# The dense stage of an attention and expert kernel on two scaled fp16 parts in place of float32r parts, always in pairs of token tiles

## The chip, the cores and the metric

The kernel runs on one core of a Trainium2 chip. The metric is device time in microseconds of one execution, as the median of several runs. The core's engines are PE (TensorE, matrix products; PEld is its weight load), DVE (VectorE), ACT (ScalarE), POOL (GpSimd) and SP (SyncE, which issues most transfers).

## What is computed

Three layers, one after the other, on 4 x 768 = 3072 tokens:

```python
# attention: 4 batches, 8 heads, 768 positions, 64 per head; a key is kept where it is one of the
# first 8, or lies less than 96 behind the query; ALiBi-like bias, softmax
x = attention(q, k, v)                                    # 3072 x 512
h = np.maximum(np.maximum(x @ w1, x @ w2), x @ w3)        # dense stage: 512 -> 768, three weights
x2 = h @ w_out                                            # 768 -> 512
e_idx = argmax(x2 @ w_gate)                               # one of 8 experts for each token
out = gate * sigmoid(x2 @ w_output_gate)[e_idx] * (relu(x2 @ w1[e_idx]) @ w2[e_idx])   # 512 -> 1024 -> 512
```

The dense weights w1, w2, w3 and w_out come as float64, so a row of weights is first put together to float32 by integer operations. All results must have about float32 accuracy. The kernel gets there with products of operands in two parts: x = xh + xl, w = wh + wl, and x w is taken as xh wh + xl wh + xh wl, three passes of the PE in place of one.

## The kernel before

A planner in Python (class `Plan`) writes the order of the work. Every piece of work is a generator that yields requests: `need` (facts that must hold), `take` (a free buffer of a kind), `op` (an instruction on an engine, with an estimated duration and the buffers that it reads and writes). `Plan.run` picks, again and again, the operation that can start earliest by its estimates, plus a hold time, ties by rank, and emits it. Each engine then runs its instructions in exactly this order, and the waits between engines follow from the data. A transfer is issued by SP in the same fixed order, with an estimated rate. If something comes later than estimated, the engine stands at it, whatever else would be ready.

The work in order of time:

- **Attention**, 24 units of 128 queries (`a_T`, `a_v`, `a_scores`, `a_trans`, `a_out`), up to about 467 us. A unit's result goes to memory (`xd`) in rows of one token tile (128 tokens).
- **Weight rows** (`load_row`, `convert`): 18 rows of 128 x 768 (w1, w2, w3) or 128 x 512 (w_out). A raw row is loaded straight to where the finished row will stand; two raw rows share a tile, so the finished parts can be written only when both partner rows have been read (`read`, m ^ 1). ACT scales the high words, DVE puts the bits together in three operations, ACT writes the high part, POOL the low part, both float32r (4 bytes).
- **Dense stage** (`m_load`, `m_1`, `m_max`, `m_2`): the first 16 token tiles go in eight pairs, the last 8 in two quads (four tiles). `m_load` loads a tile's x, transposes it on the PE and splits it (`split_T`: high part by ACT, low part by DVE). `m_1` makes the three products: in a pair each pass has 256 moving columns, in a quad 512; 216 passes for a pair, and 216 for a quad. `m_max` takes the banks: ACT copies the first product, DVE takes the maximum with the second and the third, then ACT and POOL or DVE split the hidden values into two parts. Three banks (`mbank`) are in turn. `m_2` multiplies with w_out, 18 passes of 512 columns for each tile. A pair's transposed x and hidden values have one buffer each (`xT`, `hh`); a quad's have one each too (`xTq`, `hhq`), in memory that is free only after attention (`open_m2`).
- **Routing** (`m_route`): a tile's expert choice, and an indirect transfer of its rows to the expert's region (`xs`). After 16 routed tiles `choose` fixes the order of the experts; when all 24 are routed, `lists` makes the lists of the loop. `pad_rows` writes twelve blocks of padding rows after attention.
- **Expert weights ahead of the loop** (`stage`, `split`): 16 pieces of 128 x 1024 float32 for the first two experts are loaded into staging buffers (`ws`) and split into fp16 parts, high part times 2^13 by ACT or DVE, low part by DVE. Two staging buffers exist at first; six more lie where w3 stood and come when the last `m_1` is through with w3 (`more_ws`). The finished parts of piece 4 and later lie where w1 and w2 stood, so their splits wait for the end of the last passes with w1 (pieces 4 to 9) or w2 (the rest).
- **Prologue and loop** (`pro_load`, `pro_1`, `pro_next`, `step`): the first 256 tokens of the first expert, with fp16 passes of 256 columns (L1631) and 512 (L1606), then a loop of 13 steps up to 957 us.
- **End**: a check over the collected range sums sets a flag; where it fails, `general_moe` computes all again in float32 (`tc.If(again > 0)`, L1862). `acc` holds sums of the low parts of the fp16 splits, `lows` the maxima of 64 columns of rows.

The shape of a dense pass, the lines that the change turns on:

```python
for d in range(KD):
    yield op(PE, pe(nt * P, 3), [xT, W_AT[j]], [bank])
    for n, (part, X) in enumerate(((0, xh), (0, xl), (1, xh))):
        nc.tensor.matmul(pj[:, f2, :], lhsT=w_at(j, part, d)[:, fs], rhs=X[:, d, :], ...)
```

Of the kernel before, what the change touches and what calls it, by code (L numbers as in the profile page):

```python
# [9 lines left out]
F32 = mybir.dt.float32  # L10
# [41 lines left out]
HS = 2.0**15  # L52
LOW = 2.0**-10
# [323 lines left out]
def local_attention_moe_kernel(  # L377
# [28 lines left out]
    NPAIR = NTILE // 2 - 4  # L406
    CHUNKS = [range(2 * c, 2 * c + 2) for c in range(NPAIR)] + [range(n, n + 4) for n in range(2 * NPAIR, NTILE, 4)]
    NCHUNK = len(CHUNKS)
# [14 lines left out]
    lows = cp.tile([P, NTILE + 6], F32, name="lows")  # L423
# [4 lines left out]
    hh_t = [mo.tile([P, KF, 2 * P], F32R, tag=f"hh{n}", name=f"hh{n}") for n in range(2)]  # L428
    WN = 2 * KD * FF
    WC = [FF, FF, FF, D]  # L430
    W_RAW, W_FIT = {}, {}
    for j in (0, 1, 2, 3):
        for n in range((KD if j < 3 else KF) // 2):
            W_RAW[j, n] = big.tile([P, 4 * WC[j]], F32, tag=f"w{j}{n}", name=f"raw{j}{n}")
    RAW = [W_RAW[j, c // 2][:, c % 2 * 2 * WC[j] : (c % 2 + 1) * 2 * WC[j]].bitcast(I32) for j, _, c in wrows]

    def w_at(j, part, c):
        if (j, c // 2) not in W_FIT:
            W_FIT[j, c // 2] = big.tile([P, 4 * WC[j]], F32R, tag=f"w{j}{c // 2}", name=f"w{j}{c // 2}")
        at_ = 2 * (c % 2) + part  # L440
        return W_FIT[j, c // 2][:, at_ * WC[j] : (at_ + 1) * WC[j]]
# [6 lines left out]
    with tc.manual_schedule(engines={mybir.EngineType.SP, mybir.EngineType.Activation}):  # L448
# [3 lines left out]
        for j, src in enumerate((q, k, v)):  # L452
# [7 lines left out]
            if j:  # L460
                _, w, c = wrows[j - 1]
                nc.sync.dma_start(out=RAW[j - 1], in_=w[c * P : (c + 1) * P, :].bitcast(I32))
# [130 lines left out]
    cp.tile([P, LINE // 2], F32, name="to_line")  # L593
    stock("hh", [hh_t])
# [102 lines left out]
    place = [Buf(t) for t in RAW]  # L697
    w_left = [KD, KD, KD, KF]

    def load_row(m):  # L700
        j, w, c = wrows[m]
        if m > 1:
            yield need(("row", m - 1), *([("k", ROW_LOAD[m])] if ROW_LOAD[m] >= 0 else []))
            yield dma(P * WC[j] * 8, [place[m - 2]], [place[m]])
            nc.sync.dma_start(out=RAW[m], in_=w[c * P : (c + 1) * P, :].bitcast(I32))
        state("row", m)
        plan.add(convert(m), (2, ROW_KEY[m], 9, m), HOLD_W if m < 2 * KD else HOLD_V)

    def convert(m):
# [4 lines left out]
        low, high = RAW[m][:, ::2], RAW[m][:, 1::2]  # L714
# [3 lines left out]
        yield op(ACT, act(n), [wt], [wb])  # L718
        nc.scalar.mul(out=wf, in_=high.bitcast(F32), mul=REBIAS)
# [1175 lines left out]
```

## Time and profile before

| what | value |
|---|---|
| time, median of 3 runs | 975.76 us (975.08 to 976.81) |
| the profiled execution: its time | 978.62 us |
| its span, first to last instruction | 977.1 us |
| PE busy | 897.1 us, 92% |
| PEld busy | 747.5 us, 77% |
| DVE busy | 678.2 us, 69% |
| ACT busy | 491.6 us, 50% |
| POOL busy | 223.0 us, 23% |
| mean granted PE clock | 0.968 |
| bytes moved | 160.9 MB, 165 GB/s |

How to read it: the shares are means over stages with different limits, so the stretches have to be looked at one by one. Matmuls are pipelined: a pass's record reaches from its start to its end, and the next one starts long before that, so the time that a pass costs is the distance from start to start in an unbroken burst, not its duration. The granted clock is the share of 2.4 GHz that the PE got; it has two levels, 1.0 and 0.5 (1.2 GHz). An engine's idle time is followed by the name of what ended it.

### The profile page before, as it was taken

The page shows a single profiled execution, that of the slowest core. Times are in us where ns is not written, and L with a number is a line of the kernel's source. Part 1 is how long each engine was busy: PE and PEld are TensorE (multiplying, and loading weights), DVE is VectorE, ACT ScalarE, POOL GpSimd, SP SyncE. Part 2 cuts the span into 40 slices and gives each one's busy share as a digit, 9 for nine tenths or more (in the row PEclk, how much of TensorE's full clock was granted, in tenths as well). Part 3 has the DMA queues.
Part 4 walks back from the last instruction along what each step waited for, and adds up shares of the span by engine and source line. Part 5 has one row for each costly group of instructions (what it writes and reads, how often), then busy time and mean ns, then how long its engine had stood idle before and what let it go on. Part 6 is the DMA issues. An engine that isn't in the chain of part 4 may idle for free. (4 is left out here: it accounts for less than half of the span.)

```text
span 977.1 us, 23443 instructions
## 1 busy us (share of the span) xinstructions
PE 897.1 (92%) x8305; PEld 747.5 (77%) x8305; DVE 678.2 (69%) x2101; ACT 491.6 (50%) x1070; POOL 223.0 (23%) x245
## 2 busy tenths in 40 slices
PE   2496898999899999999899998998999999999992
PEld 2385787998889898989778877777777777777770
DVE  6979876677768778776253535764777777777773
ACT  4767664676566656565121311332555444545551
POOL 3544322243222132120000010010222323222222
PEclk9997899999999999999899999998999999999996
DMA  7889286596875757664722102417777777776775
GB/s 207 234 221 235 57 154 131 132 170 139 159 143 113 162 130 158 137 137 100 200 92 60 33 33 74 142 44 248 223 227 229 240 240 238 239 251 218 224 228 185
DMA packets 222807, 160.90 MB, mean 165 GB/s; under 512 B 181344, under 2 KB 181344, under 8 KB 222724
## 3 DMA queue, kind: packets, MB, share of 16 engines
q1 hardware_dynamic: 218562, 147.23, 58.3%
q0 software_dynamic: 4160, 12.62, 3.4%
q8 instruction: 45, 0.74, 0.3%
q14 instruction: 38, 0.31, 0.1%
q10 hardware_dynamic: 2, 0.00, 0.0%
HBM read 118.56 MB, written 23.11 MB: 145 GB/s over the span
## 5 line engine op out<-in xcount | busy, mean ns | idle before, releaser
L1093 PE MATMUL bank<-xT,w 128*128 128x256 f32 x1728 | 234.8, 291 | 1.5 <-ACT xT L1037 1.0
L1093 PEld LDWEIGHTS bank<-xT,w 128*128 128x128 f32 x1728 | 217.9, 194 | 8.4 <-ACT xT L1037 3.2
L1606 PE MATMUL bank<-we,hE 128*128 128x512 f16 x672 | 147.3, 379 | 0.0
L1606 PEld LDWEIGHTS <-hE 128*128 128x128 f16 x672 | 65.7, 98 | 76.2
L950 ACT ACTIVATE sp<-sp,mn 128x232 f32<-128x232 f32 (+1 forms) x192 | 90.4, 472 | 53.1 <-DVE mn L943 46.4
L1093 PE MATMUL bank<-wq,w 128*128 128x512 f32 x432 | 103.7, 400 | 3.1 <-DVE hm L1115 3.1
L1595 ACT ACTIVATE hm<-bank 128x512 f32<-128x512 f32 x56 | 33.4, 597 | 140.1 <-PE bank L1652 94.3
L1093 PEld LDWEIGHTS bank<-wq,w 128*128 128x128 f32 x432 | 82.3, 193 | 20.7 <-DVE hm L1115 3.5
L198 DVE SCALAR_TENSOR_TENSOR we<-ws_more,we 128x1024 f16<-128x1024 f32 x81 | 96.9, 1222 | 0.2
L1115 DVE TENSOR_TENSOR hm<-hm,bank 128x512 f32<-128x512 f32 x72 | 49.4, 686 | 64.5 <-PE bank L1093 63.9
L1255 POOL DMA_INDIRECT xs<-x2r,di x24 | 24.8, 1032 | 281.0 <-DVE x2r L1252 150.2
L1529 ACT ACTIVATE we<-ws_more 128x1024 f16<-128x1024 f32 x80 | 79.9, 1047 | 0.3 <-DMA ws_more<-in_moe_w_dram 0.3
L1153 PE MATMUL bank<-w,hh 128*128 128x512 f32 x288 | 78.1, 417 | 0.0
L1652 PEld LDWEIGHTS <-we 128*128 128x128 f16 x1248 | 73.1, 100 | 5.2 <-ACTq L1835 2.0
L1652 PE MATMUL bank<-xE,we 128*128 128x128 f16 x1248 | 74.4, 222 | 2.0 <-DVE xE L198 1.8
L1652 PE MATMUL bank<-xE,wp 128*128 128x128 f16 x1248 | 71.8, 219 | 0.0
L1652 PEld LDWEIGHTS <-wp 128*128 128x128 f16 x1248 | 70.8, 98 | 0.1
L943 DVE CUSTOM_DVE_ANT_0 sp<-bank,bias 128x232 f32<-128x232 f32 x160 | 60.1, 389 | 11.4 <-PE bank L919 11.0
L820 POOL TENSOR_SCALAR qkn<-qkn,vs 128x512 f32<-128x512 f32 x23 | 38.2, 1662 | 118.9 <-DVE vs L815 50.0
L919 PE MATMUL bank<-k,qh 64*128 64x232 f32 (+1 forms) x384 | 44.5, 321 | 20.8 <-ACT k L893 17.4
L1153 PEld LDWEIGHTS bank<-w,hh 128*128 128x128 f32 x288 | 54.1, 198 | 10.6
L193 POOL TENSOR_TENSOR seen<-wf,dco 128x1 f32<-128x1 f32 x14 | 13.2, 940 | 199.7 <-DVE wf L1611 199.7
(276 smaller groups left out, 1526.4 us busy)
## 6 DMA issues: line engine op xcount, KB each, us to landing
ws_more<-in_moe_w_dram SPq DMA_DIRECT2D x87, 512.0 KB, 4.0
bias<-in_moe_w_dram SPq DMA_DIRECT2D x21, 512.0 KB
ws<-in_moe_w_dram SPq DMA_DIRECT2D x20, 512.0 KB
raw<-in_moe_w_dram SPq DMA_DIRECT2D x12, 768.0 KB
x2r<-xs SPq DMA_DIRECT2D x30, 257.0 KB, 2.7
qkn<-in_q_dram SPq DMA_DIRECT2D x23, 256.0 KB
qkn<-in_k_dram SPq DMA_DIRECT2D x23, 256.0 KB
qkn<-vd SPq DMA_DIRECT2D x23, 256.0 KB
```

The costliest lines, as they stand in the source:

```text
L198: nc.vector.scalar_tensor_tensor(out=out, in0=x, scalar=scale, in1=high, op0=ALU.mult, op1=ALU.subtract, accum_out=total)
L820: nc.gpsimd.tensor_scalar(out=vf, in0=vf, scalar1=scale, scalar2=None, op0=ALU.mult)
L919: nc.tensor.matmul(sc[j][:, hp, :nw_], lhsT=x, rhs=y, start=(n < 2), stop=(n >= len(terms) - 2))
L943: nc.vector.tensor_tensor_reduce(out=o[:, g:], in0=x[:, g:], in1=bias[:, pr, n0 + g :], scale=scale, scalar=low, op0=ALU.add, op1=ALU.min, ...
L950: nc.scalar.activation(out=o, in_=o, func=AF.Exp, scale=-1.0, bias=mn[:, h : h + 1], accum_out=sm[:, h : h + 1])
L1093: nc.tensor.matmul(pj[:, f2, :], lhsT=w_at(j, part, d)[:, fs], rhs=X[:, d, :], start=(d + n == 0), stop=(d == KD - 1 and n == 2))
L1115: nc.vector.tensor_max(out=hv, in0=hv, in1=pj)
L1153: nc.tensor.matmul(bank.t, lhsT=X[:, f, t * P : (t + 1) * P], rhs=w_at(3, part, f), start=(f + n == 0), stop=(f == KF - 1 and n == 2))
L1529: nc.scalar.mul(out=h, in_=s.t, mul=XS)
L1595: nc.scalar.activation(out=rows, in_=bank.t, func=AF.Relu, scale=HS / XS**2)
L1606: nc.tensor.matmul(py, lhsT=at(A_), rhs=w, start=(f + m == 0), stop=(last and m == 2))
L1652: nc.tensor.matmul(pg[:, f, :], lhsT=W[d][B_][:, fs], rhs=xT[A_][:, d, :], start=(d + m == 0), stop=(d == KD - 1 and m == 2))
```

## The change

- The dense stage's operands are fp16 parts: x times 2^13 (`XS`), the weights times 2^16 (`WS`), hidden values times 2^13. The three passes per product stay. The evictions take the scale out again: ACT's copies become scaled copies, DVE's maximum becomes one operation with a scale and a maximum. The low part of x comes from `low_of`, which leaves a sum beside it.
- All 24 tiles go in pairs: twelve pairs, no quads, no `xTq` and `hhq`. fp16 takes half the room: `xT` and `hh` become two buffers each. The last pair runs in the same order as the others.
- Finished weight rows have a place of their own (`W16`). Raw rows go through a ring of eight buffers (`raw`); a row waits until the buffer of the eighth row before it has been read. Partner rows don't wait for each other.
- The fp16 parts of the 16 expert pieces lie in the ring's memory (24 half pieces) and in `wp0` (8), so their splits need no dense weight to be done with. Nine staging buffers (`ws`) from `open_m2` on; `more_ws` goes. `stage` waits for the issue of the last x load as well.
- `pro_1` puts its hidden values where w1 stood and waits for the last `m_1`.
- Range checks: for each weight row DVE takes the largest magnitude of the finished high part (`widest`, after attention unit 6 + m mod 6), ACT's first step takes an absolute value with a sum; for each x tile DVE takes a maximum over 64 columns. All sums lie in one tile, `chk`; the final check has four more DVE operations.
- The branch to `general_moe` gets `preferred_fallthrough_block=False`.

```diff
-    NPAIR = NTILE // 2 - 4
-    CHUNKS = [range(2 * c, 2 * c + 2) for c in range(NPAIR)] + [range(n, n + 4) for n in range(2 * NPAIR, NTILE, 4)]
+    NCHUNK = NTILE // 2
+    CHUNKS = [range(2 * c, 2 * c + 2) for c in range(NCHUNK)]
...
-    hh_t = [mo.tile([P, KF, 2 * P], F32R, tag=f"hh{n}", name=f"hh{n}") for n in range(2)]
+    hh_t = [mo.tile([P, 2 * KF, 2 * P], F16, name=f"hh{n}") for n in range(2)]
...
+    W16 = [big.tile([P, 2 * KD * FF], F16, tag=f"w{j}", name=f"w{j}") for j in range(4)]
+    NRAW = 8
+    raw_t = [big.tile([P, 2 * FF], F32, tag=f"raw{n}", name=f"raw{n}") for n in range(NRAW)]
...
+            place[m] = yield take("raw")
             yield dma(P * WC[j] * 8, [place[m - 2]], [place[m]])
...
+    def widest(m, h):
+        yield need(("o", QT + m % QT))
+        n = h.shape[1]
+        yield op(DVE, dve(n))
+        nc.vector.tensor_reduce(out=chk[:, A_W + m : A_W + m + 1], in_=h, axis=AX.X, op=ALU.max, apply_absolute_value=True)
...
-        yield op(ACT, act(n), [wt], [wb])
-        nc.scalar.mul(out=wf, in_=high.bitcast(F32), mul=REBIAS)
+        yield op(ACT, act(n) + 0.2, [wt], [wb])
+        nc.scalar.activation(
+            out=wf, in_=high.bitcast(F32), func=AF.Abs, scale=REBIAS * 4.0, accum_out=chk[:, A_C + m : A_C + m + 1]
+        )
...
-        state("read", m)
-        yield need(("read", m ^ 1))
+        give("raw", wt)
...
+            for n in range(2):
+                t = mo.tile([P, 2 * KD, 2 * P], F16, tag=f"xT{n}", name=f"xT{n}")
+                xb = Buf([t[:, :KD], t[:, KD:]])
...
-        yield from split_T(xb, xb.t, M["xT", p], slice(t * P, (t + 1) * P))
+        yield op(DVE, 0.2, [xb], [])
+        nc.vector.tensor_reduce(out=chk[:, A_L + n : A_L + n + 1], in_=xb.t[:, :NLOW], axis=AX.X, op=ALU.max)
...
+        nc.scalar.mul(out=h, in_=pt, mul=XS)
+        yield psum(dve(D) + 0.07, [bank, xT], [xT])
+        low_of(nc, l, pt, XS, h, chk[:, n : n + 1])
...
-                    yield op(PE, pe(nt * P, 3), [xT, W_AT[j]], [bank])
+                    yield op(PE, pe16(nt * P, 3), [xT, W_AT[j]], [bank])
...
-            nc.scalar.copy(out=hm.t.rearrange("p (a b) -> p a b", a=nb), in_=pj)
+            nc.scalar.mul(out=hm.t.rearrange("p (a b) -> p a b", a=nb), in_=pj, mul=1.0 / WS)
...
-            nc.vector.tensor_max(out=hv, in0=hv, in1=pj)
+            nc.vector.scalar_tensor_tensor(out=hv, in0=pj, scalar=1.0 / WS, in1=hv, op0=ALU.mult, op1=ALU.max)
...
-            yield op(PE, pe(512, 3), [hb, W_AT[3]], [bank])
+            yield op(PE, pe16(512, 3), [hb, W_AT[3]], [bank])
...
-        for t in (bias_t, m2.tile([P, FE], F32, name="ws0")):
+        for t in (bias_t, *[m2.tile([P, FE], F32, name=f"ws{n}") for n in range(8)]):
...
-        yield need(("es",))
+        yield need(("es",), ("x", X_SEQ[-1] - 1))
...
-        yield need(("px",), ("hh", NCHUNK - 1), *[("split", d) for d in range(KD)])
+        yield need(("px",), ("mm", len(passes) - 1), *[("split", d) for d in range(KD)])
...
-        facts = [("left", 0 if n < 10 else 1)] if n > 3 else []
-        plan.add(split(plan, n, [("m2",)] + facts), (5, 2, n), HOLD_S)
+        plan.add(split(plan, n, [("m2",)]), (5, 2, n), HOLD_S)
...
-    with tc.If(again > 0):
+    with tc.If(again > 0, preferred_fallthrough_block=False):
```

## Rows read from the trace of the kernel before

**Rows 1.** Busy us by stretch: PE, PEld, DVE, ACT, POOL; granted clock, DMA share, GB/s

```profile
0.00:120.00 120.00, 73.53 (x634) 66.80 (x635) 97.72 (x245) 79.48 (x176) 49.40 (x62) 0.91 0.74 194
180.00:467.00 287.00, 284.55 (x2927) 263.01 (x2926) 212.67 (x769) 176.80 (x492) 67.21 (x68) 1.00 0.67 138
467.00:670.00 203.00, 193.54 (x1020) 153.19 (x1017) 105.42 (x365) 50.70 (x110) 15.75 (x46) 0.96 0.30 90
```

**Rows 2.** Longest wait of PE, 120 to 465 us: total us, times, longest

```profile
PE bank L1000 <- DMA aT<-nat: 3.2, 2, 2.4
```

**Rows 3.** Timeline of PE, 455 to 670 us: start, duration, what, count, idle before

```profile
454.74 6.88 PE L1093 MATMUL bank<-xT,w 128*128 128x256 f32 x56
461.46 0.87 PE L1000 MATMUL bank<-va,aT 128*128 128x64 f16 x24
...
477.85 1.09 PE L1034 MATMUL bank<-ident,wf 128*128 128x128 f32 x4 [2.98 <-DMA wf<-xd]
478.59 6.82 PE L1153 MATMUL bank<-w,hh 128*128 128x512 f32 x18
...
496.70 43.81 PE L1093 MATMUL bank<-wq,w 128*128 128x512 f32 x192
540.35 1.03 PE L1034 MATMUL bank<-ident,x 128*128 128x128 f32 x8
...
607.49 14.02 PE L1093 MATMUL bank<-wq,w 128*128 128x512 f32 x48 [3.11 <-DVE hm L1115]
...
623.34 4.37 PE L1153 MATMUL bank<-w,wq 128*128 128x512 f32 x18
627.54 0.60 PE L1034 MATMUL bank<-ident,x2r 128*128 128x128 f32 x4
...
649.15 5.73 PE L1631 MATMUL bank<-xE,wp 128*128 128x256 f16 x51
654.71 10.52 PE L1606 MATMUL bank<-we,hE 128*128 128x512 f16 x48
665.07 0.60 PE L1574 MATMUL bank<-ident,x2r 128*128 128x128 f32 x4
```

**Rows 4.** Groups of PE by line: count, busy us, mean ns, idle before

```profile
L1093 PE MATMUL bank<-xT,w 128*128 128x256 f32 x1728 | 234.8, 291 | 1.5 <-ACT xT L1037 1.0 <-DVE xT L193 0.3
```

**Rows 5.** Busy time of line 1093 alone, first stretch: us, PE, PEld, clock, DMA

```profile
0.00:120.00 120.00, 40.44 (x273) 37.89 (x274) 0.91 0.74 194
```

**Rows 6.** Timeline of all engines, 470 to 500 us: one of SP's lines

```profile
474.80 4.78 SPq L692 DMA_DIRECT2D xs<-x2r  x7
```

**Rows 7.** Timeline of all engines, 596 to 612 us: lines of SP and DVE

```profile
599.61 0.39 SPq L1506 DMA_DIRECT2D bias<-in_moe_w_dram  x1
...
603.36 0.69 DVE L1531 TENSOR_SCALAR we<-bias 128x1024 f16<-128x1024 f32 x1 [1.90 <-DMA bias<-in_moe_w_dram]
604.09 1.23 DVE L198 SCALAR_TENSOR_TENSOR we<-bias,we 128x1024 f16<-128x1024 f32 x1
```

**Rows 8.** Busy time by slices of 20 us, as rows 1: one slice

```profile
600.00:620.00 20.00, 16.89 (x63) 13.33 (x62) 13.38 (x24) 2.78 (x4) 0.00 (x0) 0.83 0.53 158
```

**Rows 9.** The raw rows' tile: count, ns min/median/max, first and last start

```profile
L719 ACT ACTIVATE x2r<-raw x10: 651/885/934, 11.4 to 107.7; 128x768 f32<-128x768 f32 x6, 128x512 f32<-128x512 f32 x4
L705 SPq DMA_DIRECT2D raw<-in_moe_w_out_dram x6: 432/715/3287, 72.9 to 80.5; - x6
```

**Rows 10.** Timeline of all engines, 655 to 672 us: one of DVE's reduces

```profile
659.67 0.42 DVE L1441 TENSOR_REDUCE rowf<-sel 1x30 f32<-1x270 f32 x1
```

**Rows 11.** Groups of DVE and of ACT by line, as rows 4

```profile
L1171 DVE TENSOR_REDUCE lows<-x2r 128x1 f32<-128x64 f32 x24 | 5.1, 214 | 9.2 <-ACT x2r L1164 9.0
...
L802 ACT ACTIVATION_READ_ACCUMULATOR va<-qkn 128x1 f32 x23 | 4.3, 189 | 0.0
```

**Rows 12.** Line 1862, the fallback's branch: count, ns min/median/max, first and last start

```profile
L1862 ACTq COMPARE_BRANCH  x1: 72/72/72, 971.2 to 971.2; - x1
...
L1862 PEldq COMPARE_BRANCH  x1: 4381/4381/4381, 971.3 to 971.3; - x1
```

More of the change, by code (lines that the diff above doesn't have):

```diff
@@ L693, in pad_rows @@
         give("x2r", padrow)
-    place = [Buf(t) for t in RAW]
+    place = {n: Buf(t) for n, t in enumerate(raw_t[:2])}
+    stock("raw", raw_t[2:])
     w_left = [KD, KD, KD, KF]
@@ L766, in first_done @@
         if left0[0] == 3:
-            xb = Buf([mo.tile([P, KD, 2 * P], F32R, tag=f"xT{n}", name=f"xT{n}") for n in range(2)])
-            G["xT"] = xb.t
-            xb.last = 20.0
-            give("xT", xb)
+            for n in range(2):
+                t = mo.tile([P, 2 * KD, 2 * P], F16, tag=f"xT{n}", name=f"xT{n}")
+                xb = Buf([t[:, :KD], t[:, KD:]])
+                xb.last = 20.0
+                give("xT", xb)
     def a_load(u, name):
@@ L1056, in m_load @@
         if t == 0:
-            M["xT", p] = yield take(q_tag("xT", c))
+            M["xT", p] = yield take("xT")
             state("xT", p)
         yield need(("xT", p))
-        yield from split_T(xb, xb.t, M["xT", p], slice(t * P, (t + 1) * P))
+        yield op(DVE, 0.2, [xb], [])
+        nc.vector.tensor_reduce(out=chk[:, A_L + n : A_L + n + 1], in_=xb.t[:, :NLOW], axis=AX.X, op=ALU.max)
+        xT = M["xT", p]
+        bank = yield take("bank")
+        pt = bank.t.rearrange("p (a b) -> p a b", b=P)
+        for d in range(KD):
+            yield op(PE, 0.109, [xb], [bank])
+            nc.tensor.transpose(pt[:, d, :], xb.t[:, d * P : (d + 1) * P], ident)
+        h, l = [x[:, :, t * P : (t + 1) * P] for x in xT.t]
+        yield op(ACT, act(D), [bank], [xT])
+        nc.scalar.mul(out=h, in_=pt, mul=XS)
+        yield psum(dve(D) + 0.07, [bank, xT], [xT])
+        low_of(nc, l, pt, XS, h, chk[:, n : n + 1])
+        give("bank", bank)
         give("x", xb)
@@ L1080, in m_1 @@
             order = [(g, j) for j in js for g in range(KF // nb)]
-        elif p == len(passes) - 1:
-            order = [(g, j) for n in range(0, KF // nb, 3) for j in js for g in range(n, n + 3)]
         for g, j in order:
@@ L1161, in m_2 @@
         if M["hh", c, "left"] == 0:
[L1162 removed]
+            give("hh", hb)
         yield op(ACT, act(D), [bank], [x2])
[L1164 removed]
+        nc.scalar.mul(out=x2.t[:, :D], in_=bank.t, mul=1.0 / (XS * WS))
         give("mbank", bank)
@@ L1269, in w_part @@
     def w_part(e, d):
[L1271 to L1280 removed]
+        parts = []
+        for n in range(2 * (e * NPC + d), 2 * (e * NPC + d) + 2):
+            if n < 24:
+                k, at_ = divmod(n, 3)
+                if ("raw", k) not in G:
+                    G["raw", k] = big.tile([P, 4 * FF], F16, tag=f"raw{k}", name=f"we{k}")
+                t = G["raw", k]
+            else:
+                t, at_ = G["wp0"], n - 24
+            parts.append(t[:, at_ * FE : (at_ + 1) * FE])
+        return parts
     def open_m2():
@@ L1331, in open_m2 @@
         state("m2")
-    def more_ws():
-        yield need(("m2",), ("left", 2))
-        for k in range(KD // 2):
-            t = big.tile([P, 4 * FF], F32, tag=f"w2{k}", name=f"ws_more{k}")
-            for n in range(4 * FF // FE):
-                b = Buf(t[:, n * FE : (n + 1) * FE])
-                b.last = plan.free[PE] + plan.DRAIN
-                give("ws", b)
     ES_AT, LISTS_AT = Buf(None), Buf(None)
@@ L1689, in pro_load @@
         T["xT"] = xT = yield take("xT")
-        G["xE"] = [mo.tile([P, 2 * KD, 2 * P], F16, tag=f"xT{n}", name=f"xE{n}")[:, :KD] for n in range(2)]
+        G["xE"] = xT.t
         for t, xb in enumerate(xbs):
@@ L1761, in local_attention_moe_kernel @@
         b.free = b.last = 15.0
-    for b, ready in zip(place, (9.1, 12.7)):
+    for b, ready in zip(place.values(), (9.1, 12.7)):
         b.written = b.last = b.free = ready
```

110 lines of the change are left out of this document (50 added, 60 removed).

## The prediction

> **What bounds the kernel now.** I read the busy times by stretch first [rows 1]. TensorE is busy 61% of the first 120 us, 99% from 180 to 467 and 95% from 467 to 670, and its granted clock stands at 0.96 to 1.00 there (2.4 GHz but for a few us). VectorE never passes 82%: 81% in the first stretch, 74% from 180 to 467. So up to 120 us the start of attention is bound by its own chain, and from there to the end TensorE's queue is. Its waits confirm it [rows 2]: in some 345 us of attention with dense work the longest of them, for transfers, come to 3.2 us. The stretch from 670 is the expert loop, in fp16 already, which the change leaves alone. What can move are the 550 us from 120 to 670, and there the question is how long one pass of the dense stage takes.
>
> Mean durations are of no use for that, since passes overlap; I take start to start over unbroken bursts of the timeline [rows 3]. Float32r, 256 columns: 56 from 454.74 to 461.46 us, 120 ns. Float32r, 512 columns: 192 from 496.70 to 540.35, 227.3 ns. Second product, float32r, 512 columns: 18 from 623.34 to 627.54, 233.3 ns. The same trace has both fp16 forms, in the expert prologue: 256 columns, 51 from 649.15 to 654.71, 109.0 ns; 512 columns, 48 from 654.71 to 665.07, 215.8 ns.
>
> **The change part by part.** *Dense passes in fp16.* There are 1728 pair passes [rows 4], and by the loops 432 passes of the two quads (two times 216) and 432 of the second product (24 tiles times 18). 273 pair passes lie before 120 us, where TensorE waits anyway [rows 5]; I count nothing for them (bound: 273 x 11 ns = 3 us). The other 1455 give 1455 x (120 - 109) = 16.0 us. The quads' passes become twice as many of half the width: 432 x 227.3 = 98.2 us against 864 x 109.0 = 94.2 us, 4.0 us. The second product: 432 x (233.3 - 215.8) = 7.6 us. Sum 27.6 us, all on the engine that sets the end.
>
> Here a rule can be weighed. In these rows the float32r form costs 11 ns more than fp16 at 256 columns and 11.5 at 512 [rows 3]. The Trainium skill, TensorE: Matmul & The Clock Gate, section Weight-path perf modes, says that the fast weight load works for every type but FP32, so that a narrower type saves on the load. By that alone a pair pass, with a stream as short as such a load, would gain, and a 512-column pass, whose stream covers the load, would not: some 15 us in place of 27.6. The rows at 512 columns differ by type all the same, so the sum stays with them.
>
> *Two transposed inputs and two hidden buffers in place of one, pairs to the end, no quad buffers.* Two stalls hang on the old layout [rows 3]. At 474.9 the first quad's buffers have just been opened, its input rows are requested among twelve padding writes in SP's queue [rows 6], and TensorE stands 2.98 us at a transpose; the 18 second products behind it take 6.82 us where 18 take 4.37 at 623 us. At 604 VectorE stands in expert splits whose rows have not landed, because two staging buffers are all there is before the third weight matrix is free [rows 7]; the eviction behind them is late, TensorE waits 3.11 us, and the next 48 passes take 14.02 us where 48 x 227.3 ns are 10.9. The granted clock of 600 to 620 us is 0.83 [rows 8], a third of that time at half clock (1.2 GHz): the idle time is paid twice. Sum 3.0 + 2.4 + 3.1 + 3.1 = 11.6 us. With pairs and two buffers the next input is fetched a pass ahead, and with nine staging buffers and free places for all 16 expert pieces the splits need not follow the last dense passes. The staging gets a wait for the last input row's request; that comes when the third pass before the last begins, so three passes with their second products (216 x 0.109 + 36 x 0.216 = 31 us each) are left for 16 pieces, which at two buffers came every 3.8 us [rows 7]. Queued behind that wait on SP are the prologue's rows, which need the same fact already. I count the whole 11.6 us; bounds 0 and 11.6.
>
> *Weight rows through eight ring buffers.* Row m now waits for the conversion of row m - 8. Rows 12 to 17 are requested at 72.9 to 80.5 us and conversions begin at 11.4 and end at 107.7 [rows 9], about 5.7 us apart, so rows 4 to 9 are read by about 35 to 65 us. Nothing; if one is late, the next attention rows stand behind it in SP's queue, bound 3 us.
>
> *More VectorE work.* 18 maxima over 128x768 fp16. The trace has no such row. Reduces of 64 and 270 elements take 0.21 and 0.42 us [rows 10, 11], 1.0 ns per element more, so about 0.93 us; bounds are the 0.69 and 1.23 us of the split's two 1024-element operations [rows 7]. I take 0.93, by the operation of its own kind: 17 us, after attention's units 6 to 11. Input checks 14 x 0.21 and accumulator reads come to 4 us in the same stretch. VectorE in 120 to 467 us, at its 74% some 257 us [rows 1], becomes 278 of about 325 us, 85%. TensorE has three banks of 24 passes each in hand, so one delay of 0.9 us is hidden; without that cover all 21 us would count. Between 0 and 21 I take 8, nearer to nothing, since VectorE's idle time in that stretch is mostly its waiting for TensorE. The scaled evictions and the fp16 splits keep their element counts: nothing.
>
> *ScalarE.* An accumulator read of 189 ns with each of 18 conversions [rows 11], 3.4 us on an engine that is busy 66% of that stretch [rows 1]: nothing, bound 3.4 us.
>
> *The end.* The final check grows by four small VectorE operations, 0.5 us on the path. The fallback's branch gets another layout: now TensorE's sequencer needs 4.38 us for the jump where ScalarE's needs 0.07 [rows 12]. If the usual way falls through, I expect 3.5 us less; bounds 0 and 4.4.
>
> **Sum:** 27.6 + 11.6 + 3.5 - 0.5 - 8 = 34.2 us. The profiled execution took 978.62 us (span 977.1 and 1.5 around it), 0.3% over the median of 975.76; that offset stays, and the sum comes off the median: 941.6, rounded to **941 us**.
>
> **The rivals.** *Stalls replaced, not removed.* TensorE's order is fixed by a plan with estimated transfer times, and both stalls come from transfers later than planned. New ones can stand elsewhere. Then 27.6 + 3.5 - 0.5 - 8 = 22.6 is left, 953 us. Against it: inputs are fetched a pass ahead.
>
> *VectorE becomes the bound in attention.* For it: at 81% it left TensorE starved in the first 120 us [rows 1]. If it can't pass 80%, 278 us of work need 347 us in place of 325, and 22 us are lost in place of 8: 27.6 + 11.6 + 3.5 - 0.5 - 22 = 20, 956 us, and with part of the stalls back some 960 us. Against: the start has few dense passes to fill its chain; later eight tiles are in hand.
>
> *The passes don't get faster.* Something that the prologue's burst doesn't show could hold them at 120 ns: 11.6 + 3.5 - 0.5 - 6 = 8.6, 967 us.
>
> *The 512-column product doesn't gain.* If a float32r load hides under a 512-column stream and what the rows show there belongs to something else, the second product stays at 233.3 ns: 7.6 us less, 949 us. That is where the skill's rule on the load leads; against it stand the 215.8 ns of the same form in fp16.
>
> *Slower: the clock.* An idle time of TensorE of 3 us cost 2.4 to 3.1 us more behind it, 6 us in all [rows 3, 8]. With a faster TensorE and a fuller VectorE such a thing can come once per attention unit, at the transfers that attention waits for already [rows 2]. From 7 on (7 x 6 = 42 = 34 + 8) the gain is gone; with ten it is 976 - 42 + 60 = 994 us. Against: at present two short waits for transfers in 347 us. The Trainium skill, same page, section HAM oscillation, describes this falling back between bursts; the trace agrees at the two places above.
>
> **How the numbers follow.** Forecast 0.56 (its own range 932 to 950), the product alone not gaining 0.04. Nothing lost to VectorE and the start better as well, below 930: 0.06. Stalls replaced 0.12, VectorE 0.12, passes as before 0.03. All these are faster: 0.93. Gain just eaten, 0.02. Slower by the clock, 0.05. A difference of 0.2% (2 us) is about what can be told from none. The range 926 to 962 leaves out the passes that stay, the clock, and the outer ends of the rest.
>
> **What would show it.** Right: bursts of dense passes at 109 ns and second products at 216; no TensorE idle time where attention ends or before the last passes; expert splits spread over the last 100 us before the loop; attention's end near 445 us; the branch near 0.1 us on TensorE; the loop's steps unchanged. Wrong: TensorE below 95% busy between 120 and 445 us with VectorE above 88%; a granted clock below 0.95 there; or passes at 120 ns.

## The result and the profile after

The changed kernel takes 932.6 us (median, 931.4 to 934.1), the kernel before on the same chip 976.3 (975.1 to 979.7): a ratio of 0.955, 95% interval 0.952 to 0.958. Forecast were 941 us and 926 to 962. The time lies in the range, but the gain is 43.7 us and not 34.2, and it has another make-up than the sum.

The profiled execution took 932.76 us (span 931.1). Busy time by stretch, columns as in [rows 1]:

```profile
0.00:120.00 120.00, 76.48 (x709) 64.49 (x710) 97.61 (x260) 81.72 (x196) 49.96 (x63) 0.83 0.75 195
120.00:180.00 60.00, 54.39 (x503) 39.84 (x501) 45.43 (x196) 35.11 (x106) 16.46 (x20) 0.91 0.77 153
180.00:470.00 290.00, 288.16 (x3108) 235.29 (x3106) 229.03 (x820) 183.20 (x503) 72.73 (x75) 1.00 0.65 139
470.00:624.00 154.00, 149.30 (x1204) 114.36 (x1200) 88.39 (x317) 46.24 (x95) 13.44 (x40) 0.99 0.34 109
624.00:911.00 287.00, 285.85 (x3223) 211.73 (x3224) 216.34 (x554) 150.37 (x195) 72.65 (x50) 1.00 0.74 238
```

The expert loop begins at 624.5 us where it began at 669.6, so 45.1 of the 46.0 us by which the two profiled spans differ are won ahead of it. From 180 us on TensorE is as full as it was [rows 1]. Two things in the first lines are new: 709 TensorE instructions before 120 us in place of 634, and 120 to 180 us, where TensorE stands for 5.6 us and the clock is 0.91. In the kernel before it stood for 2.7 us there:

```profile
120.00:180.00 60.00, 57.30 (x511) 50.55 (x510) 41.19 (x157) 34.33 (x98) 15.08 (x18) 0.94 0.75 142
```

The bursts, timeline of TensorE (start, duration, what, count):

```profile
502.20 16.53 PE L1123 MATMUL bank<-xT,w 128*128 128x256 f16 x150
518.57 0.60 PE L1087 MATMUL bank<-ident,x 128*128 128x128 f32 x4
...
556.47 4.05 PE L1180 MATMUL bank<-w,hh 128*128 128x512 f16 x18
560.36 0.60 PE L1054 MATMUL bank<-ident,x2r 128*128 128x128 f32 x4
```

150 first products take 16.37 us from start to start, 109.1 ns each, and 18 second products 3.89 us, 216 ns. [rows 3] had 120, 227.3 and 233.3 ns. This is the step that the prediction rested on.

**A cost that the sum had missed: the first pass of a burst.** In attention the dense passes come in short bursts between other instructions. The first block of lines is the kernel before, the second the changed one, timeline of TensorE:

```profile
314.46 0.60 PE L1093 MATMUL bank<-xT,w 128*128 128x256 f32 x3
314.90 0.87 PE L1000 MATMUL bank<-va,aT 128*128 128x64 f16 x24
```

```profile
439.44 0.49 PE L1123 MATMUL bank<-xT,w 128*128 128x256 f16 x3
439.77 0.60 PE L1087 MATMUL bank<-ident,wf 128*128 128x128 f32 x4
440.20 1.46 PE L1180 MATMUL bank<-w,hh 128*128 128x512 f16 x6
```

Three passes take 0.44 us before (3 x 0.120 would be 0.36) and 0.33 after (3 x 0.109). Counted over the bursts after 120 us, the time from the first pass of a burst to its second has a median of 202 ns before for the first product (120 within a burst) and 316 for the second (231). 152 of 160 bursts show it; the other eight stand right behind float32r passes of the other product. The excess sums to 12.6 us, without three bursts at half clock. After it is 109 and 216 ns, and 2 of 172 bursts show more than 11 ns, both at half clock.

Not all of that is won. Where float32 transposes stand ahead of the burst, the kernel before starts the burst's first pass 29 ns (median) behind the last transpose, and the changed kernel 109 ns. The last lines above show it: four transposes take 0.43 us, 4 x 0.109. Before, eight take 0.79 and not 0.87:

```profile
322.48 1.04 PE L1034 MATMUL bank<-ident,x 128*128 128x128 f32 x8
323.27 0.94 PE L1153 MATMUL bank<-w,hh 128*128 128x512 f32 x3
```

From the last transpose to the second pass there is thus no gain but the cadence. 55 of the 172 bursts are of this kind: 55 x 80 ns, 4.4 us, come back, and some 8 us are left.

**A stall that moved: the expert pieces.** After attention, at 490 us. First TensorE, then ScalarE, then SP's queue (timelines, idle time in brackets):

```profile
489.68 0.82 PE L1180 MATMUL bank<-w,hh 128*128 128x512 f16 x3
492.83 0.39 PE L1226 MATMUL bank<-two,lg 32*128 32x16 f32 x2 [2.32 <-ACT lg L1221]
```

```profile
491.57 1.06 ACT L1541 ACTIVATE we<-bias 128x1024 f16<-128x1024 f32 x1 [3.47 <-DMA bias<-in_moe_w_dram]
492.54 0.24 ACT L1221 COPY lg<-bank 32x128 f32<-32x128 f32 x1
```

```profile
473.54 7.38 SPq L699 DMA_DIRECT2D xs<-x2r  x12
480.96 0.79 SPq L1075 DMA_DIRECT2D x<-xd  x1
481.80 0.50 SPq L1075 DMA_DIRECT2D wf<-xd  x1
483.69 0.34 SPq L1518 DMA_DIRECT2D bias<-in_moe_w_dram  x1
```

The first expert piece is issued at 483.69, behind the twelve padding writes that stood ahead of the old stall's input rows as well [rows 6], and lands 7.9 us later. ScalarE's order has the split of that piece (line 1541) ahead of the routing copy (line 1221) for which TensorE waits. 480 to 500 us has TensorE busy 17.7 us at a clock of 0.91, 2.3 us of idle time and 1.8 of half clock (1.2 GHz):

```profile
480.00:500.00 20.00, 17.68 (x119) 11.82 (x117) 7.67 (x30) 8.57 (x17) 0.80 (x1) 0.91 1.02 287
```

**A stall that is new: no dense pass at hand.** Timeline of TensorE, 146 to 174 us:

```profile
145.82 1.15 PE L1123 MATMUL bank<-xT,w 128*128 128x256 f16 x9
...
157.38 1.47 PE L1180 MATMUL bank<-w,hh 128*128 128x512 f16 x6
...
167.20 0.66 PE L887 MATMUL bank<-ident,qkn 128*128 128x128 f32 x4 [1.12 <-DVE xo L1026]
...
169.89 1.11 PE L1087 MATMUL bank<-ident,x 128*128 128x128 f32 x4 [1.78 <-DVE cnt L1262]
172.42 1.11 PE L887 MATMUL bank<-ident,qkn 128*128 128x128 f32 x4 [1.42 <-DVE xT L200]
173.33 1.06 PE L1123 MATMUL bank<-xT,w 128*128 128x256 f16 x4
```

The first products of the second pair end at 147, their second products at 159, and the next first product starts at 173.3. What it waits for are the transposes of the sixth tile (line 1087, at 169.89), which stand behind the routings of the third and fourth tile (lines 1054, 1214 to 1246) in the order. In between TensorE follows the short chains of attention and routing, waits for VectorE, and loses its clock.

### The profile page after: what moved, and what is told of

It reads as the page before. It is cut to its first block, busy times and chain, and to the rows that moved or that the text cites. A ratio compares the mean times of both kernels' runs of the same rounds, so it can differ in the third digit from the quotient of the medians.

```text
span 931.1 us, 24358 instructions
## 1 busy us (share of the span) xinstructions
PE 854.8 (92%) x8737; PEld 665.8 (72%) x8737; DVE 682.5 (73%) x2162; ACT 496.6 (53%) x1092; POOL 228.1 (24%) x250
## 5 line engine op out<-in xcount | busy, mean ns | idle before, releaser
L1123 PE MATMUL bank<-xT,w 128*128 128x256 f16 x2592 | 307.1, 276 | 2.7 <-ACT xT L1090 1.4
L1123 PEld LDWEIGHTS <-w 128*128 128x128 f16 x2592 | 250.5, 99 | 38.8 <-issue 4.3
L1664 PE MATMUL bank<-xT,we 128*128 128x128 f16 x2496 | 144.0, 219 | 1.6 <-ACTq L1846 1.4
L1664 PEld LDWEIGHTS <-we 128*128 128x128 f16 x2496 | 141.6, 98 | 5.0 <-ACTq L1846 1.6
L1618 PEld LDWEIGHTS <-he 128*128 128x128 f16 x672 | 65.7, 98 | 76.2
L1180 PE MATMUL bank<-w,hh 128*128 128x512 f16 x432 | 102.8, 379 | 0.0
L1618 PE MATMUL bank<-we,he 128*128 128x512 f16 x360 | 80.0, 379 | 0.0
L1618 PE MATMUL bank<-wp,he 128*128 128x512 f16 x312 | 69.5, 379 | 0.0
L200 DVE SCALAR_TENSOR_TENSOR wp<-ws,wp 128x1024 f16<-128x1024 f32 x56 | 66.1, 1217 | 0.0
L200 DVE SCALAR_TENSOR_TENSOR we<-ws,we 128x1024 f16<-128x1024 f32 x49 | 59.6, 1220 | 0.0
```

The costliest lines, as they stand in the source:

```text
L200: nc.vector.scalar_tensor_tensor(out=out, in0=x, scalar=scale, in1=high, op0=ALU.mult, op1=ALU.subtract, accum_out=total)
L1180: nc.tensor.matmul(bank.t, lhsT=X[:, f, t * P : (t + 1) * P], rhs=w_at(3, part, f), start=(f + n == 0), stop=(f == KF - 1 and n == 2))
L1618: nc.tensor.matmul(py, lhsT=at(A_), rhs=w, start=(f + m == 0), stop=(last and m == 2))
L1664: nc.tensor.matmul(pg[:, f, :], lhsT=W[d][B_][:, fs], rhs=xT[A_][:, d, :], start=(d + m == 0), stop=(d == KD - 1 and m == 2))
```

## Experiments

All times are medians in us; "before" is the kernel before, run beside it on the same chip, and its median moved between 972.5 and 977.0, so the ratios are what is compared. Two profiles of one order of work put the loop's start at 624.5 and 626.9: a difference of 2 us between two traces says nothing by itself.

| run | time | before | ratio, 95% interval |
|---|---|---|---|
| the change | 932.6 | 976.3 | 0.955 (0.952 to 0.958) |
| before, with breaks | 987.5 | 977.0 | 1.011 (1.007 to 1.016) |
| after, with breaks | 938.7 | 977.0 | 0.961 (0.957 to 0.965) |
| before, pairs alone | 970.5 | 972.5 | 0.998 (0.995 to 1.000) |
| after, two early staging buffers | 932.3 | 972.5 | 0.958 (0.954 to 0.962) |
| after, no maxima | 929.2 | 972.5 | 0.953 (0.950 to 0.957) |
| after, old branch layout | 934.0 | 977.0 | 0.954 (0.950 to 0.959) |
| after, later splits | 931.7 | 977.0 | 0.953 (0.949 to 0.957) |
| after, single buffers | 918.8 | 972.5 | 0.943 (0.939 to 0.947) |
| after, one hidden buffer | 936.6 | 975.1 | 0.960 (0.956 to 0.963) |
| after, one input buffer | 927.8 | 975.1 | 0.950 (0.947 to 0.953) |
| after, five ring buffers | 925.8 | 975.1 | 0.948 (0.945 to 0.951) |
| after, order alone | 926.9 | 974.3 | 0.951 (0.948 to 0.954) |

**1 and 2. Does a burst's start cost anything, and in fp16?** The same line goes into both kernels:

```diff
                 fs = slice((nb * g + f2) * P, (nb * g + f2 + 1) * P)
+                nc.tensor.matmul(pj[:, f2, 0:1], lhsT=ones, rhs=ones[:, 0:1], start=True, stop=True)
                 for d in range(KD):
```

> The kernel before with one tiny bfloat16 product (one column) put ahead of each of the 180 accumulation groups of the first product; the group that follows overwrites what it wrote, so nothing that is computed changes. Theory (first pass of a burst): in the kernel before the first float32r pass after any other instruction holds the next pass up by about 90 ns, so each tiny product costs its own 25 to 30 ns and another 90 ns: about 120 ns x 157 groups outside the first 120 us = 19 us, up to 22 us if the start-up pays too; the time is 993 to 999 us, and the start-to-start time from the first pass of a group to its second is about 210 ns where the others show 120. Rival (the bursts cost nothing, and the missing 12 us lie elsewhere): 30 ns x 157 = 5 us, 979 to 983 us, and all start-to-start times of a group are 120 ns.

> The changed kernel with the same tiny product ahead of each of its 216 accumulation groups of the first product. Theory (only float32r passes pay at a burst's start): 25 to 30 ns x about 188 groups outside the first 120 us = 5 to 6 us, at most 8; 937 to 941 us, and the first pass of a group follows its neighbours at 109 ns like the others. Rival (any change of the operand stalls TensorE, in fp16 as well): 120 ns x 188 = 23 us, about 955 us. If this kernel loses about 5 and the kernel before about 19, the difference, some 13 to 14 us for 157 to 188 breaks, is the price of a burst's start in float32r alone.

Timelines of TensorE, the kernel before with breaks, then the changed kernel with breaks:

```profile
480.39 0.18 PE L1090 MATMUL bank<-ones 128*128 128x1 bf16 x1
480.43 1.67 PE L1094 MATMUL bank<-xT,w 128*128 128x256 f32 x12
481.94 0.18 PE L1090 MATMUL bank<-ones 128*128 128x1 bf16 x1
```

```profile
504.05 0.17 PE L1120 MATMUL bank<-ones 128*128 128x1 bf16 x1
504.07 1.47 PE L1124 MATMUL bank<-xT,w 128*128 128x256 f16 x12
505.38 0.17 PE L1120 MATMUL bank<-ones 128*128 128x1 bf16 x1
```

Before, one break with its twelve passes takes 1.55 us, 110 ns more than 12 x 120; after 1.33 us, 22 ns more than 12 x 109. Over all breaks that the trace shows whole, the first pass is followed after 201 ns before (128 breaks) and after 108 ns (148 breaks). The price of a burst's start in float32r is shown, and fp16 has none behind such a bfloat16 product; behind float32 transposes only the traces speak (above). The changed kernel lost 6.1 us, as expected. The kernel before lost 10.5 and not 19: the price per break was right, but its two old stalls shrank with the fuller TensorE (granted clock 1.00 from 470 to 640 us for 0.96, 1.00 from 120 to 180 for 0.94). So a cost on the engine that bounds can be paid in part out of its own idle time.

**3. Were the two old stalls a matter of the buffers?** Two runs: pairs alone in the old kernel, and the changed kernel with the old, late staging.

```diff
-    NPAIR = NTILE // 2 - 4
+    NPAIR = NTILE // 2
```

> The kernel before with all 24 tiles as twelve pairs and no quads: float32r, single buffers, two early staging buffers as before. It undoes nothing of the change but does its pair part alone. Cadence: 864 pair passes at 120 ns for 432 quad passes at 227.3 ns is 5.5 us more. Theory (the first stall hung on the quads' buffers being opened late; pairs have theirs): 3.0 + 2.4 us of the stall at 475 us go, the staging stall stays: 976 to 977 us. Rival (single buffers stall at each pair, whatever its size): 982 to 990 us. If pairs alone were the gain, it would be 965 us or less.

```profile
470.00:600.00 130.00, 130.00 (x978) 121.58 (x978) 54.70 (x195) 31.84 (x73) 7.17 (x22) 1.00 0.25 78
600.00:640.00 40.00, 39.73 (x313) 36.83 (x311) 25.66 (x79) 16.72 (x31) 3.71 (x8) 1.00 0.43 146
```

Busy times of this run, columns as in [rows 1]: with pairs alone TensorE is idle for 0.3 us from 470 to 640, single buffers and two staging buffers or not. Both stalls are gone, not one, and the loop starts 7.0 us earlier, near the 11.6 of the stalls less 5.5 of cadence. That compares two traces from two chips, and the one of the kernel before is on the long side (978.6 us). In the medians on one chip it is 2.0 us, interval -0.3 to 4.7, so that the stalls were worth some 7.5 us there and not 11.6. Both stalls came with the quads. Pairs also draw a new order, though, and whether it was the quads' buffers or only their order was not separated.

```diff
-        for t in (bias_t, *[m2.tile([P, FE], F32, name=f"ws{n}") for n in range(8)]):
+        ws_t = [bias_t, *[m2.tile([P, FE], F32, name=f"ws{n}") for n in range(8)]]
+        for t in ws_t[:2]:
...
+    def more_ws():
+        yield need(("m2",), ("left", 2))
+        for t in ws_t[2:]:
...
```

> The changed kernel, but only two of the nine staging buffers for expert weights are given at the end of attention; the other seven when the last first-product pass of the third weight matrix has been issued, as the kernel before did. The prediction's step: the late staging is one of the two stalls, 3.1 us of wait and 3.1 us of half clock: 938 to 940 us, with a wait of TensorE of 2 to 4 us near the end of the dense passes. Rival 1 (staging was never the cause once pairs and double buffers are there): 932 to 933 us. Rival 2 (few pieces early are even better, since the first expert split no longer stands where ScalarE waited at 490): that wait of 2.3 us is still there or gone by the place of the first split; if it is gone and the end pays nothing, 929 to 931 us.

Rival 1: 932.3 us. The pieces then go one by one through two buffers from 486 to 562 us, and that is early enough. The wait for the routing copy is still there, 1.6 us. Having seven of the nine staging buffers early brings nothing.

**4. What do VectorE's maxima cost?**

```diff
-        plan.add(widest(m, h), (6, m), 0.4)
```

> The changed kernel without the 18 maxima over the weights' upper parts (15.1 us of VectorE between 180 and 400 us); the range check on the weights is left out with them. The plan orders the rest anew. The prediction's step: 21 us of added VectorE work cost 8, of which these 15 to 17 us are 6: 926 to 927 us. Theory after the trace (VectorE was 79% busy from 180 to 470 and TensorE waited 1.8 us there): they cost 0 to 1 us, 931.5 to 933 us, and TensorE stays at 99% from 180 to 470. Rival on the other side (the other order brings a new wait): above 935 us with a wait of 2 us or more that the changed kernel does not have.

```profile
180.00:470.00 290.00, 288.08 (x3116) 233.85 (x3114) 213.53 (x798) 186.94 (x506) 65.03 (x72) 1.00 0.67 138
470.00:600.00 130.00, 130.00 (x1073) 102.42 (x1072) 73.56 (x245) 42.49 (x86) 11.36 (x36) 1.00 0.35 114
```

VectorE has 15.5 us less to do from 180 to 470, and TensorE is busy 288.1 us there as before: the maxima cost nothing that shows. The loop starts 3.6 us earlier. The plan drew another order, in which the wait at 490 is gone (second line), but 3.0 of the 3.6 us are there already at attention's end (467.6 for 470.6), so the gain has no single place.

**5. The branch.**

```diff
-    with tc.If(again > 0, preferred_fallthrough_block=False):
+    with tc.If(again > 0):
```

> The changed kernel with the branch's layout as it is by default (the argument that chooses the fall-through block is taken out); nothing else differs. The prediction's step gave the layout 3.5 us: then 936 us, and the span from the final product to the end is 3 to 4 us longer than the 5.7 us of the changed kernel. Theory after the trace: TensorE's sequencer still shows a branch of 3.7 us at the end, so the layout gives 0.9 us at most: 932.5 to 934 us, and the end part is 5.7 to 6.6 us. Rival: the layout does nothing at all and the 0.9 us came from elsewhere: end part 5.7 us, 932.6 us.

The longest branch on TensorE's sequencer, the changed kernel and then this run (count, ns min/median/max):

```profile
L1877 PEldq COMPARE_BRANCH  x2: 83/1909/3735, 926.1 to 926.4; - x2
```

```profile
L1877 PEldq COMPARE_BRANCH  x1: 3354/3354/3354, 929.8 to 929.8; - x1
```

From the last product to the end are 5.8 us with the new layout and 5.9 with the old one. The layout is worth nothing: the long jump is there in both, in the new one at the second of two branches.

**6. Is the stall at 490 the split's place in ScalarE's order?** The plan is told that a piece lands 5 us later:

```diff
             nc.sync.dma_start(out=view(s.t), in_=src)
+            s.written += 5.0
             staged.append(s)
```

> The changed kernel with the plan told that each expert weight piece lands 5 us later than it reckoned; the transfers are issued as before, the expert splits are only put later in ScalarE's and VectorE's order. Theory (new stall): ScalarE stood at the first expert split until its piece had landed behind the twelve padding writes, and TensorE waited 2.3 us for the routing copy queued behind that split at 492.8, after which its clock was half for one slice (0.91 in 480 to 500). With the split later the wait goes: 2.3 us and up to 1.9 us for the clock, 3 to 4.2 us less, 928.5 to 930 us, and no wait of TensorE over 1 us between 480 and 500. Rival (the stall is taken up elsewhere: TensorE would meet another wait, or a split that comes too late holds up the prologue): within 1 us of the changed kernel, 932 to 933 us.

```profile
480.00:500.00 20.00, 20.00 (x154) 14.46 (x153) 7.94 (x31) 5.31 (x13) 0.00 (x0) 1.00 1.04 294
```

The wait is gone and 154 TensorE instructions fit where 119 did; from the end of attention to the loop are 149.8 us for 153.9. The time is 0.9 us less where 3 to 4.2 were expected, inside what runs of one order differ by. The cause of the wait is shown, its price only by the trace.

**7. Do two buffers help?**

```diff
-    stock("hh", [[t[:, :KF], t[:, KF:]] for t in hh_t])
+    stock("hh", [[t[:, :KF], t[:, KF:]] for t in hh_t[:1]])
...
-                give("xT", xb)
+                if n == 0:
+                    give("xT", xb)
```

> The changed kernel with one buffer in place of two for the transposed input and one for the hidden layer; pairs, fp16 passes and staging stay. Theory of the prediction (the buffers remove the stall after attention): TensorE waits at every pair after attention for transposes and splits, 4 or 5 pairs with 1 to 3 us each and some half clock behind them: 938 to 946 us. Rival (the second products of the pair before, 36 x 0.216 = 7.8 us, cover the next pair's input and the hidden layer is free by then): 932 to 935 us.

918.8 us: neither theory. Taking the second buffers away makes the kernel faster than the change itself, and the intervals do not touch. The line to read is 120 to 180 us (further down): TensorE is full there, and the wait at 490 is missing too. So what had been held for a cost of missing buffers was none, and 12 us (by the ratios) to 14 (by the medians of two chips) lay in something else. The next three runs ask whether that is the buffers or only the order that the plan makes when they change.

> The changed kernel with one buffer for the hidden layer and still two for the transposed input. With both single the time was 918.8 us and TensorE was busy 59.7 of the 60 us from 120 to 180, where the changed kernel shows 54.4. Theory (order, not buffers: between 150 and 173 the changed kernel has no dense pass ready, since its plan puts two routings ahead of the sixth tile's transposes; in this kernel's order those transposes come before the second of these routings): no stretch without dense passes at 160 to 180, TensorE 58 to 60 us busy there, 919 to 925 us. Rival (the input's second buffer is what costs): as the changed kernel, 931 to 934 us and TensorE about 54.5 us busy from 120 to 180.

> The changed kernel with one buffer for the transposed input and two for the hidden layer. Its order has the sixth tile's transposes after the third routing's last products, as late as the changed kernel. Theory (order): the stretch without dense passes is there, TensorE 54 to 56 us busy from 120 to 180, and 928 to 934 us. Rival (a single input buffer holds the dense work back and so lets attention run ahead): 58 us or more busy there, 919 to 925 us.

In the third the buffers stay and five ring buffers take the place of eight:

```diff
-    stock("raw", raw_t[2:])
+    stock("raw", raw_t[2:5])
```

> The changed kernel with five ring buffers for weight rows in place of eight; both input buffers and both hidden buffers stay. The prediction gave the ring nothing either way (bound 3 us): by it 931 to 935 us. Theory (order): with fewer buffers the rows are requested later and the plan orders the rest anew; the sixth tile's transposes then come before the second routing's last products, so the stretch without dense passes at 160 to 180 is gone although all buffers of the dense stage are there twice: TensorE 58 us or more busy from 120 to 180, and 920 to 927 us. Rival (two buffers cost by themselves): 54.5 us busy there, 931 to 935 us. Rival 2 (the ring matters: TensorE waits for weights in the first 120 us): 335 dense passes before 120 us become fewer than 300, and the time is above 936 us.

Busy time from 120 to 180 us, in this order: single buffers, one hidden buffer, one input buffer, five ring buffers.

```profile
120.00:180.00 60.00, 59.70 (x620) 46.44 (x618) 46.56 (x191) 39.03 (x112) 20.12 (x22) 1.00 0.74 152
```

```profile
120.00:180.00 60.00, 57.56 (x574) 44.86 (x573) 44.10 (x186) 36.64 (x104) 17.84 (x22) 0.97 0.63 142
```

```profile
120.00:180.00 60.00, 56.25 (x535) 41.73 (x533) 44.99 (x195) 35.65 (x105) 16.68 (x20) 0.94 0.73 151
```

```profile
120.00:180.00 60.00, 60.00 (x603) 46.40 (x602) 44.98 (x199) 38.46 (x108) 14.95 (x20) 1.00 0.69 146
```

The sixth tile's transposes start at 154.8, 156.8, 165.6 and 158.9 us in them, and at 169.9 in the changed kernel. The three before 160 us have TensorE busy 57.6 to 60.0 us, the two after it 54.4 and 56.3. One input buffer came out just outside what the theory of the order expected for it (56 us, 928 us), and short of the rival's 58 us. Five ring buffers with everything else twice do as well as single buffers in that stretch. It is the order, then, not the number of buffers, and the ring has no worth of its own beyond five.

The traces say what the order costs. From 120 us to the loop's start, TensorE's idle time and what the half clock cost (1 less the granted clock, times its length) are together 19.4 us in the change, 4.7 with single buffers, 23.4 with one hidden buffer, 13.1 with one input buffer and 8.3 with five ring buffers. The rest of the time to the loop is 481 to 488 us in all five: the same work, with more or less standing between.

One hidden buffer won that stretch and still took 936.6 us, a miss. It met a worse stall after attention, waits of TensorE and ScalarE's timeline:

```profile
PE bank L1226 <- ACT lg L1221: 9.2, 1, 9.2
```

```profile
525.87 0.60 ACT L1191 ACTIVATE x2r<-bank 128x512 f32<-128x512 f32 x1 [9.85 <-DMA xs<-x2r,di]
526.36 0.24 ACT L1221 COPY lg<-bank 32x128 f32<-32x128 f32 x1
```

There ten padding writes were issued behind the expert pieces, as late as 490.7 to 511.5 us, and held one of the three row buffers meanwhile. ScalarE stood at line 1191 for another, until a scatter that GpSimd had issued only at 519.0 had read it, and the routing copy stood behind. GpSimd had waited 15.0 us before it, and the profile ends that wait with an expert piece that SP issued at 511.8, behind those padding writes; why the scatter hung on it was not traced.

**8. The order alone.** All buffers as in the change, two edits to the plan (the second is that of 6):

```diff
-        yield need(("wg",))
+        yield need(("wg",), *([("xT", 2, 1)] if tile_ in (2, 3) else []))
...
+            s.written += 5.0
```

> The changed kernel with all its buffers and all its work, and two edits to the order alone: the routings of the third and fourth tile may be planned only once the sixth tile's input is transposed and split, and the plan reckons every expert weight piece 5 us later, as in an earlier run. Theory (the last 10 us of the change are order: two stalls of TensorE, at 160 to 180 and at 490, that no buffer asks for): the stretch without dense passes from 150 to 173 gets shorter by what the two routings took, some 4 to 6 us with the half clock behind it, TensorE 57 us or more busy from 120 to 180, and the wait at 490 is gone (3 to 4 us): 922 to 927 us. Rival (the stalls only move, since the work that is put off holds up something later): 930 to 934 us, with a new wait of 2 us or more between 180 and 500. Rival 2 (only fewer buffers help, as the run with single buffers): 930 to 934 us with TensorE about 54.5 us busy from 120 to 180.

```profile
120.00:180.00 60.00, 56.37 (x573) 42.30 (x572) 46.29 (x193) 37.27 (x109) 14.87 (x19) 0.94 0.75 155
...
480.00:500.00 20.00, 20.00 (x159) 14.67 (x157) 9.68 (x45) 9.18 (x19) 2.33 (x6) 1.00 0.75 284
```

926.9 us, at the upper end of what was expected: 5.7 less than the change by the medians of two chips, 3.3 by the ratios, whose intervals just overlap. The loop starts 6.3 us earlier, and idle time and half clock ahead of it are 13.0 us for 19.4. The transposes came at 164.3 and not at 169.9, and TensorE is busy 56.4 us from 120 to 180 where 57 were expected, so a part of the first stall is left; the second one is gone.

## Why the prediction was right, and where it was off

*The cadence* (27.6 us) was right: 109.1 and 216 ns, by the same rows 26.5 us (1455 x 11 = 16.0, the quads 4.0, and 432 x 15 = 6.5, as second products before had a median of 231 ns). The Trainium skill (TensorE: Matmul & The Clock Gate, Weight-path perf modes) has the fast weight load on for full loads of every type but FP32. The prediction's reading of that rule, by which the 512-column product would gain nothing, did not decide here: it went from 231 to 216 ns. The "some 15 us" given with it do not follow from the rows; without the second product the sum is 20.0, as the rival has it.

*The burst starts* are a term that was left out, 12.6 us on the dense passes and some 8 net of what the transposes give back. The rows were there: the long bursts in [rows 3] were chosen because they are unbroken, and that is just what hides this cost. The shorter bursts of attention, where most passes lie, were never timed.

*VectorE* was the worst term in size: 8 us forecast, nothing measured. The work itself was judged well:

```profile
L723 DVE TENSOR_REDUCE chk<-w x18: 670/941/948, 180.5 to 400.5; 128x1 f32<-128x768 f16 x12, 128x1 f32<-128x512 f16 x6
```

(count, ns min/median/max, first and last start.) 0.94 us where 0.93 were forecast, 15.1 us in all; VectorE came to 79% and not 85%. But TensorE waited for nothing in it that shows, and run 4 has TensorE as full without the maxima. The reason given for "nearer to nothing" held all the way to nothing.

*The first 120 us* were counted at nothing with a bound of 3 us. 336 dense passes lie there in place of 273, 63 x 0.109 = 6.9 us of work done early. No run shows why; it is not the ring, since 319 passes lie there with five buffers. Most of it was given back at once: from 120 to 180 us TensorE lost 2.9 us more to idle time than before and 1.8 to the clock, with no dense pass at hand until the sixth tile came. The early passes don't force that: with five ring buffers 319 lie before 120 us, and TensorE is full behind them.

*The two old stalls* (11.6 us) did go, but the cause was half wrong. Pairs alone remove both (run 3); nine early staging buffers and double buffers, which the prediction credited, bring nothing (runs 3 and 7). And the rival "stalls replaced" was half true as well: the wait at 490 us costs 4.1 us by the same mechanism, a transfer that lands later than the plan reckoned, behind the same padding writes.

*The branch* (3.5 us) was wrong: run 5 gives the layout nothing. Before, the jump was 4.38 us [rows 12], in the changed kernel 3.7. The prediction took the layout of the code for the reason of the long jump, without a row that showed the other layout.

*Attention's end* was forecast near 445 us and is at 470.6 (467.2 before). The plan gave the time that the passes freed to more dense passes: 1863 of 2592 first products lie before 470 us, where it had been 1701 of the pairs and no quad.

Ahead of the loop the account can be closed from the busy times of 120 us to the loop's start, the kernel before and the changed one:

```profile
120.00:669.57 549.57, 535.10 (x4448) 466.63 (x4447) 359.27 (x1290) 261.83 (x699) 98.04 (x132) 0.98 0.54 120
120.00:624.46 504.46, 491.85 (x4807) 389.50 (x4804) 363.26 (x1333) 264.55 (x702) 102.63 (x135) 0.99 0.57 132
```

Idle time fell from 14.5 to 12.6 us, and what the half clock cost from 10.9 to 6.8. So all stalls, old and new together, won 6.0 us of the 11.6. The other 39.1 of the 45.1 us are less work to do there: 26.5 of cadence and 6.9 done early. That leaves 5.7 for the burst starts, where counting them gave some 8; the 2 us between are open.

The forecast of 34.2 was right by sign, by range and in its main term. That the total came so near is in part luck: the terms missed by +8 (VectorE), +6 (burst starts), +7 (start), -1 (cadence), -6 (stalls) and -2 (end and branch), 12 us in all, which lead to the 46.0 between the two traces; the medians show 43.7. The slower rival, the clock, did not come where dense work is at hand: 1.00 from 180 to 470 us. Single buffers start the loop 6.5 us before five ring buffers, with the same rows from 120 to 180: 3.6 of it are idle time and half clock, nearly all after 470 us, and the rest stays open.

## What to carry to other kernels

Time an operation in the bursts in which it really runs, short ones too; an unbroken burst shows the cadence and hides the cost of each start. Count what stands ahead of the burst as well: a part of that cost can move there. In a kernel whose order is made by a plan, every change to buffers or durations draws a new order, and with such changes this kernel moved between 919 and 937 us with the same work (an edit of the order alone was worth 3 to 6): look for stretches where the bounding engine has nothing at hand before crediting or blaming the buffers. Ask of every removed stall what stands in the same queue next; here the padding writes stood ahead of the old stall and of the new one.

## What the hardware showed that was not expected

A float32r pass that follows an instruction of another kind on TensorE holds the next pass up, mostly by some 80 ns (152 of 160 bursts; behind float32r passes, none). An fp16 pass holds up none, but behind float32 transposes it starts itself some 80 ns later (109 for 29 ns). The weight loads fit that (groups of PEld by line: busy us, mean ns), before and after:

```profile
L1093 PEld LDWEIGHTS bank<-xT,w 128*128 128x128 f32 x1728 | 217.9, 194 | 8.4 <-ACT xT L1037 3.2 <-issue 2.3 <-DVE xT L193 1.0
```

```profile
L1123 PEld LDWEIGHTS <-w 128*128 128x128 f16 x2592 | 250.5, 99 | 38.8 <-issue 4.3
```

A load takes 194 ns in float32r and 99 in fp16. That the longer load is what the second pass waits for is only argued: no run changed the load alone. And a jump at the end of the program costs 3.4 to 4.4 us on TensorE's sequencer in either layout of the code, where the other engines' branches take 0.05 to 0.09.
